# A block's softmax sums: scaling them on GpSimd six units earlier in its queue

## The chip, the cores and the metric

One core of a Trainium2 chip runs the whole kernel in one launch. The metric is the device time of the run in microseconds (us), here the median of three runs. The engines are TensorE (PE in the profile; its weight loads are PEld), VectorE (DVE), ScalarE (ACT), GpSimd (POOL) and SyncE (SP), which issues most of the DMAs. Each engine works through its own queue in order and waits there for semaphores of the others.

## The reference, cut to what matters

Three layers follow each other: attention with hash buckets, a mixture of experts with one expert for each token, and a SoLU layer. The change touches attention and the step from it to the experts.

```python
# attention: 2 batches x 8 heads, 768 positions, head size 64
mask = q_bucket[:, :, :, None] == k_bucket[:, :, None, :]
scores = np.where(mask, scale * q @ k.T, -1e9)
scores = scores - scores.max(-1, keepdims=True)
attn = np.exp(scores)
attn = attn / (attn.sum(-1, keepdims=True) + 1e-09)
x = attn @ v
# experts: 1536 tokens, width 512, 8 experts of width 1024
e_idx = argmax(x @ w_gate); out = gate_w * eom * (relu(x @ w1[e]) @ w2[e])
# SoLU: softmax-weighted hidden layer, layer norm, output matrix
```

## The kernel before

**Units and blocks.** Two heads form a pair (n = 0 to 7), and half of a pair's query rows form a block (j = 2n and 2n + 1, so 16 blocks). A unit is one tile of 128 query rows of one head; six units make a block, and 96 units (i = 0 to 95) make the attention loop at L976 to L996. Unit i works on the block i // 6.

**One unit.** TensorE makes the scores (`emit_s`, L558) and, in between, the transposes of the exponentials of two units earlier (`steps_t`, L597). VectorE takes the rows' maximum (`emit_max`, L568 to L572). ScalarE makes the exponential (`emit_exp`, L583), which adds up the row sums into `sums[j]`, and copies the transposes out of PSUM (L599). TensorE multiplies by v for the block before (`emit_pv`, L616).

**Background work.** Everything else hangs on a calendar written out by hand: `at(i, f, ...)` says that step f is issued in unit i, in slot 0 (behind the scores), slot 1 (behind the maximum) or slot 2 (at the unit's end). Steps with the same unit and slot are issued in the order in which they were registered. A step's place there is its place in each engine's queue.

**Finishing a block** takes these steps, counted from the block's first unit 6j: the unscaled output is read from PSUM into halves of 16 bits (`fin_hi` in 6j + 12, `fin_lo` in 6j + 13, slot 0); GpSimd adds 1e-9 to the sums and scales them into a small tile r (`fin_s`, L654, in 6j + 12, slot 2); VectorE takes the reciprocal of r (`fin_v`, L659, in 6j + 13, slot 1); TensorE multiplies by the gates (`fin_mm`, L673 to L675, in 6j + 15); VectorE scales the results with r (`fin_l`, L684, and `fin_x`, L695, in 6j + 16), and GpSimd splits the result into halves (L702, L704).

**Splitting q and k** of pair n is GpSimd's work too (`split`, L336 to L349): q is issued in unit 12(n - 1) - 1 and k in unit 12(n - 1), both in slot 2, one pair ahead of their use. SyncE's DMA transposes and copies follow (`trans`, L361, L367, L373), then TensorE's products for the buckets (`bits_a`, L509 to L515, q in 12(n - 1) + 5 and k in 12(n - 1) + 8). GpSimd further splits 16 pieces of the first experts' weights (`w_split`, L185 to L187), two in each pair. The splits are registered ahead of the finishing steps, so for even j from 0 to 10, where 6j + 12 is 12(n - 1) for n = j / 2 + 2, the queue of GpSimd has: split q, split k, `fin_s(j)`.

**The end of attention.** The last two blocks are finished by code written out behind the calendar: block 14 in units 93 and 94, block 15 in parts (query tiles 0 and 1, then 2) after the loop, at L999 to L1049. There `route_b` (L751) has GpSimd scatter three tokens' rows by indirect DMA (L762, L764), `fin_r` is `fin_s` followed by `fin_v`, and the router's steps (`route_a`, L713; `route_mm`, L732) and the gathering matmuls (`gather_mm`, L890) follow; the first expert begins on TensorE at L1143.

Of the kernel before, what the change touches and what calls it, by code (L numbers as in the profile page):

```python
# [8 lines left out]
F32 = mybir.dt.float32  # L9
# [12 lines left out]
def kernel(  # L22
# [15 lines left out]
    nc = tc.nc  # L38
# [7 lines left out]
    NP = B * HP  # L46
# [9 lines left out]
    X_S = 1024.0  # L56
    W_S = 2048.0
    G_S = 1024.0
    O_S = 16.0
# [158 lines left out]
    def setup_first():  # L218


        fi = const.tile([128, 3], F32, name="fi")
        io = const.tile([128, 1], I32, name="io")
        nc.gpsimd.iota(io, pattern=[[0, 1]], base=0, channel_multiplier=1)
        nc.gpsimd.memset(pw, 0.0)
        d = nc.vector
        d.tensor_scalar(out=io, in0=io, scalar1=31, scalar2=None, op0=ALU.bitwise_and)
        d.tensor_copy(out=fi[:, 0:1], in_=io)
        d.tensor_scalar(out=fi[:, 1:2], in0=fi[:, 0:1], scalar1=float(NBIT), scalar2=-TINY, op0=ALU.is_ge, op1=ALU.mult)
        d.tensor_scalar(out=fi[:, 2:3], in0=fi[:, 0:1], scalar1=float(2 * NBIT), scalar2=TINY, op0=ALU.is_ge,
                        op1=ALU.mult)  # L230
        d.tensor_copy(out=thr[:, 1:2], in_=fi[:, 1:2])
        d.scalar_tensor_tensor(out=thr[:, 0:1], in0=fi[:, 1:2], scalar=TINY, in1=fi[:, 2:3], op0=ALU.add, op1=ALU.add)
# [52 lines left out]
    def attention(es):  # L285
        def sbuf(name, bufs):
            return es.enter_context(tc.tile_pool(name=name, bufs=bufs))
# [9 lines left out]
        sm = sbuf("sm", 4)  # L297
# [16 lines left out]
        def at(i, f, *a, slot=2):  # L314
            bg.setdefault((i, slot), []).append((f, a))
# [231 lines left out]
        s_t, mx_t, p_t, pt, sums, pv, fin_t = {}, {}, {}, {}, {}, {}, {}  # L547
# [82 lines left out]
        lt_t = {}  # L630

        def fin_hi(j, q0=0, q1=3, on_act=False):
            if q0 == 0:
                xt = xp.tile([128, 2, SB], F16, tag="xt", name="xt")
                xf = xp.tile([128, 3, 128], F32, tag="xf", name="xf")
                r = sm.tile([128, 3, 2], F32, tag="r", name="r", bufs=2)
                fin_t[j] = lt_t[j], xt, xf, r
            o, i = fin_t[j][1][:, 0, q0 * 128:q1 * 128], pv[j, q0][:, 0:(q1 - q0) * 128]
            if on_act:
                nc.scalar.activation(out=o, in_=i, func=AF.Copy, scale=O_S)  # L640
            else:
                nc.vector.tensor_scalar(out=o, in0=i, scalar1=O_S, scalar2=None, op0=ALU.mult)
# [5 lines left out]
        def fin_a(j, q0=0, q1=3, on_act=False):  # L648
            fin_hi(j, q0, q1, on_act)
            fin_lo(j, q0, q1)  # L650

        def fin_s(j, q0=0, q1=3):
            r = fin_t[j][3][:, q0:q1]
            nc.gpsimd.tensor_scalar(out=r, in0=sums[j][:, q0:q1], scalar1=1e-9, scalar2=O_S / X_S,  # L654
                                    op0=ALU.add, op1=ALU.mult)

        def fin_v(j, q0=0, q1=3):
            r = fin_t[j][3][:, q0:q1]
            nc.vector.reciprocal(out=r, in_=r)  # L659

        def fin_r(j, q0=0, q1=3):
            fin_s(j, q0, q1)
            fin_v(j, q0, q1)
# [25 lines left out]
        def fin_x(j, q0=0, q1=3, on_act=False, on_dve=False):  # L689
# [13 lines left out]
                                        op0=ALU.mult, op1=ALU.mult)  # L703
            (nc.vector if on_dve else nc.gpsimd).tensor_tensor(out=x2[:, qs, 1, cs], in0=xf[:, qs], in1=x2[:, qs, 0, cs], op=ALU.subtract)  # L704

        fin_m = {}
        rts = {}
        parts = [(0, 3), (3, 3), (6, 3), (9, 2), (11, 1)]
# [189 lines left out]
        def gather_copy():  # L898
            xw = raw.tile([128, 1024], F32, tag="raw", name="raw").bitcast(F16)[:, 0:8 * CAP]
            xw = gx["xw"] = xw.rearrange("p (c n) -> p c n", c=8)  # L900
            for kk in range(4):
                nc.scalar.copy(out=xw[:, kk::4], in_=gx["ps"][kk][:, 0:2 * CAP].rearrange("p (a n) -> p a n", a=2))

        for n in range(1, NP):
            s0 = 12 * (n - 1)
            at(max(s0 - 1, 0), split, n, "q")
            at(s0, split, n, "k")
            at(s0 + 1, trans, n, "q")
            at(s0 + 3, trans, n, "k")
            if n + 1 < NP:  # L910
                at(s0 + 5, load, n + 1, "qk")
                at(s0 + 20, load, n + 1, "v")
            at(s0 + 5, bits_a, n, "q")
            at(s0 + 7, bits_b, n, "q", slot=0)
            at(s0 + 8, bits_a, n, "k", slot=0)
            at(s0 + 8, bits_b, n, "k", slot=1)
        JL = 2 * NP - 2
        for j in range(2 * NP):
            at(NU - 4 if j == JL else min(6 * j + 11, NU - 3), fin_pre, j)
        for j in range(JL):  # L920
            u = 6 * j + (13 if j == JL - 1 else 15)
            at(6 * j + 12, fin_hi, j)
            at(6 * j + 12, fin_s, j)
            at(6 * j + 13, fin_lo, j, slot=0)
            at(6 * j + 13, fin_v, j, slot=1)
            at(u, fin_mm, j)
            at(u + 1, fin_l, j, slot=0)
            at(u + 1, fin_x, j)
# [32 lines left out]
    with tc.manual_schedule():  # L961
        with ExitStack() as es:
            A = attention(es)
            pj = A["pj"]
            cm, rb, rg = A["cm"], A["rb"], A["rg"]
            setup_first()
            A["first"]()
            A["load"](1)
            setup_late()
            NU = A["NU"]  # L970
            bg = A["bg"]
            JL = 2 * NP - 2
            a_ = A.__getitem__
            pv, fa, tr = a_("emit_pv"), a_("fin_a"), a_("emit_t")
            due = a_("due")
            for i in range(NU):  # L976
                a_("emit_s")(i, a_("steps_t")(i - 2) if 2 <= i else iter(()))
                due(i, 0)
                a_("emit_max")(i)
                due(i, 1)  # L980
                a_("emit_exp")(i)
                jj, c = divmod(i - 8, 6)
                if 0 <= jj < JL and c % 2 == 0:
                    pv(jj, c)
                    pv(jj, c + 1)
                elif jj == JL and c < 2:
                    for x in range(3):
                        pv(JL, 3 * c + x)
                if i == NU - 3:
                    fa(JL, 0, 3, True)  # L990
                    a_("fin_r")(JL)
                if i == NU - 2:
                    a_("fin_mm")(JL)
                    a_("fin_l")(JL)
                    a_("fin_x")(JL)
                due(i, 2)  # L996
            assert not bg, bg.keys()

            J = JL + 1  # L999
            a_("route_a")(2)  # L1000
            tr(NU - 2)
            for c in range(3):
                pv(J, c, 0, 2)
            a_("route_mm")(2)
            a_("route_b")(2)
            for t in (6, 7, 8):
                a_("gather_oh")(t)
            for c in range(3, NS):
                pv(J, c, 0, 2)
            fa(J, 0, 2, True)  # L1010
            a_("fin_r")(J, 0, 2)
            a_("route_s")(2)
            tr(NU - 1)
            a_("fin_mm")(J, 0, 2)
            a_("fin_r")(J, 2, 3)
            for c in range(NS):
                pv(J, c, 2, 3)
            a_("fin_l")(J, 0, 2)
            a_("fin_x")(J, 0, 2, True)
            gm = a_("gather_mm")  # L1020
            a_("gather_ps")()
            a_("gather_first")((0, 1))
            for t in (6, 7):
                gm(t, (0, 1))
            a_("route_a")(3)
            a_("route_mm")(3, tail=True)
            fa(J, 2, 3, True)
            a_("route_b")(3)
            a_("gather_oh")(9)
            a_("fin_mm")(J, 2, 3)  # L1030
            a_("gather_first")((2, 3))
            for t in (6, 7):
                gm(t, (2, 3))
            a_("fin_l")(J, 2, 3)
            a_("route_a")(4)
            a_("route_mm")(4, (9, 10), True)
            for t in (8, 9):
                gm(t, range(4))
            a_("gather_oh")(10)
            gm(10, range(4))  # L1040
            a_("fin_x")(J, 2, 3, True, True)
            a_("route_b")(4)
            a_("gather_oh")(11)
            gm(11, range(4))
            a_("gather_copy")()
            a_("route_s")(3)
            a_("totals")()
            for x in range(3):
                a_("route_d")(x, 2, 3, 4)  # L1049
# [195 lines left out]
        for i, (kd, e, g) in enumerate(slots):  # L1245
# [18 lines left out]
            if kd == "m2" and 4 * e + g < NTILE:  # L1264
# [5 lines left out]
                    out=meta[:, :], out_offset=bass.IndirectOffsetOnAxis(ap=po, axis=0),  # L1270
# [161 lines left out]
```

## Time and profile before

| what | value |
|---|---|
| median of three runs | 562.01 us (560.13 to 562.04) |
| the profiled execution, whole time | 560.47 us |
| its span, first to last instruction | 558.7 us |
| TensorE busy | 507.0 us, 91% of the span |
| VectorE busy | 397.4 us, 71% |
| ScalarE busy | 340.2 us, 61% |
| GpSimd busy | 268.6 us, 48% |
| mean granted TensorE clock | 0.983 of full speed |

Busy time says how long an engine worked, not what bounds the kernel: attention fills the first half of the span, the experts and the SoLU layer the second, and their limits differ. Times of the trace are counted from the span's start. In a row of the timeline the first number is the start, the second the duration; a bracket at the end gives the idle time of the engine just before the row and, behind the arrow, what ended it.

### The profile page before, as it was taken

The page shows a single profiled execution, that of the slowest core. Times are in us where ns is not written, and L with a number is a line of the kernel's source. Part 1 is how long each engine was busy: PE and PEld are TensorE (multiplying, and loading weights), DVE is VectorE, ACT ScalarE, POOL GpSimd, SP SyncE. Part 2 cuts the span into 40 slices and gives each one's busy share as a digit, 9 for nine tenths or more (in the row PEclk, how much of TensorE's full clock was granted, in tenths as well). Part 3 has the DMA queues.
Part 4 walks back from the last instruction along what each step waited for, and adds up shares of the span by engine and source line. Part 5 has one row for each costly group of instructions (what it writes and reads, how often), then busy time and mean ns, then how long its engine had stood idle before and what let it go on. Part 6 is the DMA issues. An engine that isn't in the chain of part 4 may idle for free. (4 is left out here: it accounts for less than half of the span.)

```text
span 558.7 us, 10895 instructions
## 1 busy us (share of the span) xinstructions
PE 507.0 (91%) x3948; PEld 349.3 (63%) x3948; DVE 397.4 (71%) x892; ACT 340.2 (61%) x644; POOL 268.6 (48%) x355
## 2 busy tenths in 40 slices
PE   7798989899885989999799999969998999999995
PEld 5455646566553655665699999969994344444442
DVE  7866757666774866876579999999994885554530
ACT  6776767686683766886249687686652554442430
POOL 7985646676467766543528867321330112212131
PEclk9999989999998998999999999979999999999999
DMA  5577574744445442700599999999700245224251
GB/s 169 120 210 175 192 159 126 203 119 126 141 136 121 144 131 77 163 26 1 189 241 310 201 270 322 235 347 312 299 2 3 39 75 114 57 62 108 57 121 49
DMA packets 107177, 83.13 MB, mean 149 GB/s; under 512 B 80624, under 2 KB 89456, under 8 KB 107120
## 3 DMA queue, kind: packets, MB, share of 16 engines
q1 hardware_dynamic: 104816, 76.09, 51.1%
q0 software_dynamic: 2304, 6.31, 3.1%
q8 instruction: 32, 0.52, 0.4%
q14 instruction: 25, 0.20, 0.1%
HBM read 51.43 MB, written 9.97 MB: 110 GB/s over the span
## 5 line engine op out<-in xcount | busy, mean ns | idle before, releaser
L583 ACT ACTIVATE p<-s,mx 128x768 f32<-128x768 f32 x96 | 95.6, 996 | 64.4 <-DVE mx L572 46.1
L597 PE MATMUL t<-ident,p 128*128 128x128 f32 x576 | 128.1, 279 | 1.9 <-ACT pt L599 1.3
L568 DVE TENSOR_REDUCE mx<-s 128x1 f32<-128x768 f32 x96 | 91.3, 951 | 41.2 <-PE s L558 39.8
L597 PEld LDWEIGHTS t<-ident,p 128*128 128x128 f32 x576 | 78.8, 143 | 35.9 <-ACT pt L599 26.4
L599 ACT COPY pt<-t 128x384 f32<-128x384 f32 x192 | 85.4, 481 | 7.9 <-PE t L597 6.2
L558 PE MATMUL s<-k,q 128*128 128x384 f16 x192 | 60.0, 332 | 16.0 <-ACT p L583 16.0
L1154 POOL TENSOR_TENSOR hh<-hf,hh 128x448 f16<-128x448 f32 (+5 forms) x32 | 42.5, 1337 | 65.9 <-ACT hf L1153 65.8
L616 PE MATMUL v<-pt,v 128*64 128x384 f32 (+1 forms) x384 | 72.2, 500 | 1.2 <-DVE xt L646 1.2
L1298 PE MATMUL h<-wi,yT 128*128 128x512 f16 x288 | 63.8, 379 | 4.6 <-PEq L1103 2.6
L1174 PE MATMUL a<-hh,wb 128*128 128x224 f16 (+5 forms) x256 | 63.6, 251 | 0.0
L1175 PE MATMUL a<-hh,wb 128*128 128x224 f16 (+5 forms) x256 | 63.5, 251 | 0.0
L1176 PE MATMUL a<-hh,wb 128*128 128x224 f16 (+5 forms) x256 | 63.5, 251 | 0.0
L1366 PE MATMUL o<-wo,zT 128*128 128x512 f16 x288 | 63.5, 379 | 0.0
L1143 PE MATMUL a<-xw,wa 128*128 128x224 f16 (+5 forms) x224 | 56.0, 253 | 7.7 <-DVE yT L1184 6.7
L558 PE MATMUL s<-b,cm 128*128 128x384 f16 x192 | 58.2, 331 | 1.1 <-DVE b L521 1.1
L1144 PE MATMUL a<-xw,wa 128*128 128x224 f16 (+5 forms) x224 | 56.1, 254 | 0.0
L1145 PE MATMUL a<-xw,wa 128*128 128x224 f16 (+5 forms) x224 | 56.1, 254 | 0.0
L1298 PEld LDWEIGHTS <-yT 128*128 128x128 f16 x288 | 27.9, 98 | 39.0 <-DVE so L1325 3.2
L1366 PEld LDWEIGHTS <-zT 128*128 128x128 f16 x288 | 28.2, 98 | 34.0
L616 PEld LDWEIGHTS v<-pt,v 128*64 128x64 f32 x384 | 23.8, 138 | 27.6 <-issue 24.3
L1338 POOL TENSOR_TENSOR st<-st,nhalf 128x2 f32<-128x2 f32 x12 | 8.5, 706 | 66.1 <-DVE st L1337 65.9
L1314 ACT ACTIVATE ex<-h,st,csc 128x1024 f32<-128x1024 f32 x12 | 14.4, 1204 | 41.4 <-DVE st L1337 26.7
(266 smaller groups left out, 1043.6 us busy)
## 6 DMA issues: line engine op xcount, KB each, us to landing
raw<-in_moe_w_dram SPq DMA_DIRECT2D x64, 512.0 KB
raww<-in_moe_w_in_dram SPq DMA_DIRECT2D x8, 512.0 KB
raww<-in_moe_w_out_dram SPq DMA_DIRECT2D x8, 512.0 KB
xs<-raw SPq DMA_DIRECT2D x8, 448.0 KB
v<-in_v_dram SPq DMA_DIRECT2D x8, 384.0 KB
q<-in_q_dram SPq DMA_DIRECT2D x7, 384.0 KB
k<-in_k_dram SPq DMA_DIRECT2D x7, 384.0 KB
cm<-q SPq DMA_DIRECT2D x14, 96.0 KB
```

The lines of the kernel that those rows point to most:

```text
L558: nc.tensor.matmul(t[:, c, 0:SB], d[x, h][:, s], flat(d[y, h])[:, c * SB:(c + 1) * SB], start=first, stop=not first)
L568: nc.vector.tensor_reduce(out=mx[:, 0:1], in_=t[:, :, 0:SB], op=ALU.max, axis=AX.XY)
L583: nc.scalar.activation(out=p, in_=s_t.pop(i)[:, :, 0:SB], func=AF.Exp, scale=mx[:, 1:2], bias=mx[:, 2:3], accum_out=sums[j][:, qt, h:h + 1])
L597: nc.tensor.transpose(t[:, g * 128:(g + 1) * 128], p[:, c, g * 128:(g + 1) * 128], ident)
L599: nc.scalar.copy(out=pt[j, h][:, 3 * c:3 * c + 3, qt * 128:(qt + 1) * 128], in_=t[:, 0:SB].rearrange("p (g c) -> p g c", g=3))
L616: nc.tensor.matmul(pv[j, q0][64 * h:64 * h + 64, 0:w], vt[:, h, c], pt[j, h][:, c, q0 * 128:q1 * 128], start=(c == 0), stop=(c == NS - 1), ...
L1144: nc.tensor.matmul(ps[:, i, 0:n], w[:, 0, kk, fs], xw[:, KD + kk], start=False, stop=False)
L1174: nc.tensor.matmul(ps, w[:, 0, f, ds], hh[:, 0, f], start=(f == 0), stop=False)
L1175: nc.tensor.matmul(ps, w[:, 0, f, ds], hh[:, 1, f], start=False, stop=False)
L1176: nc.tensor.matmul(ps, w[:, 1, f, ds], hh[:, 0, f], start=False, stop=(f == KF - 1))
L1298: nc.tensor.matmul(ps[:, c], yT[:, a, kk, ts], w_i[:, w, kk, c * 512:(c + 1) * 512], start=(kk == 0 and a == 0 and w == 0), stop=(kk == KD ...
L1366: nc.tensor.matmul(ps, zT[:, KF * a + f], w_o[:, w, f], start=(f == 0 and a == 0 and w == 0), stop=(f == KF - 1 and a == 1))
```

## The change

`fin_s(j)` for blocks 0 to 14 moves on the calendar from unit 6j + 12 to unit 6j + 6, slot 2, and is registered ahead of the splits, so that it also comes first where unit and slot are the same. Its tile r is allocated there, with three buffers instead of two. `fin_s` of block 14 no longer stands beside its `fin_v` in unit 93 but in unit 90. For block 15 `fin_s` runs on VectorE instead of GpSimd, and its first part is issued ahead of the copies of `fa`. The reciprocal and all that reads it stay where they were.

```diff
@@ fin_hi @@
-                r = sm.tile([128, 3, 2], F32, tag="r", name="r", bufs=2)
-                fin_t[j] = lt_t[j], xt, xf, r
+                fin_t[j] = lt_t[j], xt, xf, r_t[j]
...
         def fin_s(j, q0=0, q1=3):
-            r = fin_t[j][3][:, q0:q1]
-            nc.gpsimd.tensor_scalar(out=r, in0=sums[j][:, q0:q1], scalar1=1e-9, scalar2=O_S / X_S,
+            if q0 == 0:
+                r_t[j] = sm.tile([128, 3, 2], F32, tag="r", name="r", bufs=3)
+            r = r_t[j][:, q0:q1]
+            (nc.vector if j == 2 * NP - 1 else nc.gpsimd).tensor_scalar(out=r, in0=sums[j][:, q0:q1], scalar1=1e-9, scalar2=O_S / X_S,
                                     op0=ALU.add, op1=ALU.mult)
...
         def fin_v(j, q0=0, q1=3):
-            r = fin_t[j][3][:, q0:q1]
+            r = r_t[j][:, q0:q1]
             nc.vector.reciprocal(out=r, in_=r)
...
+        JL = 2 * NP - 2
+        for j in range(JL + 1):
+            at(6 * j + 6, fin_s, j)
         for n in range(1, NP):
             s0 = 12 * (n - 1)
             at(max(s0 - 1, 0), split, n, "q")
...
             at(6 * j + 12, fin_hi, j)
-            at(6 * j + 12, fin_s, j)
...
                 if i == NU - 3:
                     fa(JL, 0, 3, True)
-                    a_("fin_r")(JL)
+                    a_("fin_v")(JL)
...
+            a_("fin_s")(J, 0, 2)
             fa(J, 0, 2, True)
-            a_("fin_r")(J, 0, 2)
+            a_("fin_v")(J, 0, 2)
```

## Rows read from the trace of the kernel before

**Rows 1.** Waits, whole span: who waited for whom, us in total, times, longest.
```profile
POOL xh L702 <- DVE xf L695: 65.1, 14, 7.0
...
DVE r L659 <- POOL r L654: 21.6, 6, 5.1
```
**Rows 2.** Timeline of one such wait, in the block of units 36 to 41: POOL, DVE, ACT.
```profile
103.73 0.83 POOL L336 TENSOR_SCALAR k<-k 128x768 f32<-128x768 f32 x1
...
108.10 0.20 POOL L654 TENSOR_SCALAR r<-sums 128x6 f32<-128x6 f32 x1
...
108.34 0.19 DVE L659 RECIPROCAL r<-r 128x6 f32<-128x6 f32 x1 [3.53 <-POOL r L654]
...
109.91 0.99 ACT L583 ACTIVATE p<-s,mx 128x768 f32<-128x768 f32 x1 [3.17 <-DVE mx L572]
```
**Rows 3.** Windows, one a block: length, then PE, PEld, DVE, ACT, POOL busy, clock, DMA.
```profile
38.97:54.76 15.79, 14.19 (x108) 8.88 (x105) 9.93 (x25) 11.54 (x25) 9.10 (x13) 1.00 0.82 183
54.76:68.59 13.83, 13.83 (x107) 8.90 (x105) 10.82 (x26) 10.95 (x24) 9.58 (x9) 1.00 0.57 191
68.59:86.72 18.13, 15.61 (x108) 9.59 (x105) 9.99 (x24) 11.72 (x25) 10.53 (x16) 0.91 0.77 189
...
100.56:117.42 16.86, 14.27 (x108) 8.89 (x105) 9.99 (x25) 11.52 (x25) 10.08 (x16) 1.00 0.69 183
...
163.68:186.20 22.52, 16.28 (x112) 9.77 (x109) 12.95 (x39) 11.73 (x25) 18.03 (x25) 0.92 0.57 151
186.20:200.03 13.83, 13.83 (x107) 8.90 (x105) 11.97 (x28) 10.95 (x24) 9.47 (x9) 1.00 0.36 121
200.03:218.73 18.70, 15.91 (x108) 9.35 (x105) 10.36 (x28) 11.84 (x27) 11.55 (x17) 0.91 0.42 103
...
232.58:245.94 13.36, 13.31 (x96) 8.67 (x93) 10.56 (x30) 11.08 (x24) 6.37 (x7) 1.00 0.52 98
```
**Rows 4.** The same columns for one microsecond behind two of the waits.
```profile
79.00:80.00 1.00, 0.95 (x3) 0.44 (x3) 0.61 (x3) 1.00 (x3) 0.00 (x0) 0.50 0.45 99
110.00:111.00 1.00, 0.00 (x0) 0.00 (x0) 0.93 (x3) 1.00 (x3) 0.00 (x0) 1.00 0.58 128
```
**Rows 5.** Timeline of PE and DVE in the block of units 60 to 65.
```profile
172.02 0.32 PE L558 MATMUL s<-k,q 128*128 128x384 f16 x1 [0.78 <-ACT p L583]
...
177.68 0.24 PE L673 MATMUL m<-rb,xt 128*128 128x160 f16 x1 [3.93 <-DVE rpr L758]
...
176.00 0.93 DVE L568 TENSOR_REDUCE mx<-s 128x1 f32<-128x768 f32 x1
```
**Rows 6.** Timeline of the end of attention: DVE, POOL, PE.
```profile
265.08 0.42 DVE L646 SCALAR_TENSOR_TENSOR xt<-v,xt 128x256 f16<-128x256 f32 x1 [0.94 <-ACT xt L640]
268.60 0.18 DVE L659 RECIPROCAL r<-r 128x4 f32<-128x4 f32 x1 [3.10 <-issue]
...
267.30 1.00 POOL L764 DMA_INDIRECT xs<-xh,slot_all  x1 [0.28 <-issue]
268.37 0.46 POOL L654 TENSOR_SCALAR r<-sums 128x4 f32<-128x4 f32 x2
...
271.13 0.18 PE L740 MATMUL v<-oh_all,upper 128*128 128x16 f16 x1 [2.45 <-DVE oh_all L727]
```
**Rows 7.** Timeline, what follows split k (SPq) and what uses it (PE).
```profile
109.83 2.58 SPq L373 DMA_TRANSPOSE b<-kl  x2
...
122.20 0.34 PE L515 MATMUL m<-b,pw 128*32 128x384 f16 x4
```
**Rows 8.** Timeline, the exponential of unit 23 (ACT) and GpSimd's split of q behind it.
```profile
69.53 0.19 ACT L583 ACTIVATION_READ_ACCUMULATOR p<-s,mx 128x1 f32 x1
...
69.70 1.79 POOL L342 TENSOR_TENSOR qs<-q,qs 128x384 f16<-128x384 f32 x2
```
**Rows 9.** Single lines: duration ns least/median/most, first and last start us, forms.
```profile
L570 DVE TENSOR_SCALAR mx<-mx x96: 153/153/156, 11.3 to 260.9; 128x1 f32<-128x1 f32 x96
...
L721 DVE SCALAR_TENSOR_TENSOR rne<-lg,rmx,iota_s x12: 213/227/885, 150.5 to 272.5; 128x8 f32<-128x8 f32 x12
```

More of the change, by code (lines that the diff above doesn't have):

```diff
@@ L704, in fin_x @@
             (nc.vector if on_dve else nc.gpsimd).tensor_tensor(out=x2[:, qs, 1, cs], in0=xf[:, qs], in1=x2[:, qs, 0, cs], op=ALU.subtract)
+        r_t = {}
         fin_m = {}
@@ L916, in attention @@
             at(s0 + 8, bits_b, n, "k", slot=1)
-        JL = 2 * NP - 2
         for j in range(2 * NP):
```

## The prediction

> **What bounds the kernel now.** I first read the waits of the whole span and looked for those that name the moved step. There is one: VectorE's reciprocal waits for GpSimd's step on the sums 6 times, 21.6 us in total, 5.1 us at the longest [rows 1]. Then I read the timeline around one of them [rows 2]. GpSimd begins with k at 103.73 and comes to the sums, 0.20 us of work, only at 108.10. VectorE stands still for 3.53 us before its reciprocal. Behind the reciprocal in VectorE's queue stands the next unit's maximum, so ScalarE's exponential starts 3.17 us late too, and TensorE, which needs that exponential out of its score buffer, runs dry behind them.
>
> Whether these stalls set the pace is seen in windows that each hold one block of six units [rows 3]. The second blocks of the pairs, where GpSimd has no split of q or k in front of the sums, take 13.83 us with TensorE busy for all of it (two such rows stand there, from 54.76 and 186.20; three more, from 86.72, 117.42 and 218.73, read 13.84, 13.83 and 13.85): there TensorE is the bound, at a clock of 1.00. The first blocks of pairs 1 to 6, each with one of the six waits, take 15.79, 18.13, 16.86, 16.86, 22.52 and 18.70 us (the fourth repeats the third, so one row stands for both) for nearly the same TensorE instructions (108 against 107; 112 in the fifth, which also routes tokens). The first block of pair 7 has nothing left to split, and takes 13.36 us, 13.31 of them busy, without the 12 small bucket products of the others. So a first block without the wait runs like a second block. Behind attention the experts start when its last step ends, and nothing of the change reaches into them; I take that half as shifted as a whole.
>
> **The change part by part.**
>
> *The move out of the split's way.* In first blocks the sums are now scaled six units, about 13.8 us, before the reciprocal, so the wait falls away. The gain of a block is its length less 13.83. Pair 1: 15.79 - 13.83 = 1.96. Pairs 3 and 4: 16.86 - 13.83 = 3.03 each. Pair 2: 18.13 - 13.83 = 4.30. Pair 6: 18.70 - 13.83 = 4.87, from which I keep back 0.2 for gating operations that only this block has, so 4.7.
>
> Pair 5 is read on its own, since there VectorE is late for a second reason, the router's work. The scores of unit 62 start only at 172.02 [rows 5], and four matmuls later, at about 173.4, the maximum can begin; in the trace it began at 176.00, right behind the reciprocal [rows 5]. The gain there is about 2.5 us, not the 5.1 of the wait, and TensorE's gap of 3.93 us before 177.68 [rows 5] shrinks to about 1.4. The rest is clock: TensorE is busy 16.28 us at a mean of 0.92 against 14.27 in the block of pair 3 [rows 3], some 1.9 us after 0.1 for four more matmuls. Sum 4.4.
>
> The blocks together: 1.96 + 4.30 + 3.03 + 3.03 + 4.4 + 4.7 = 21.4 us.
>
> Part of this is clock, not waiting. In pair 2 the granted clock is 0.50 (1.2 GHz instead of 2.4) at 79 to 80 us, after TensorE had run dry; in pair 3, after the same 3.5 us of VectorE's wait, it stays at 1.00 [rows 4]. By busy time the low clock costs 15.61 - 14.27 = 1.3 us in pair 2, 1.9 in pair 5 and 15.91 - 14.27 = 1.6 in pair 6 [rows 3], together 4.9. I take it as gone with the gaps, since the second blocks and that of pair 7, which have no such gap, ran at 1.00 [rows 3]; if it stayed, the gain would be 4.9 smaller. The Trainium skill ("TensorE: Matmul & The Clock Gate", section "HAM oscillation — how this bites in real kernels") says that idle gaps make the gate fall back to half rate and that the work behind them pays; the trace agrees in three of six gaps and shows that a gap need not do it. By that rule the dips go, and the sum stays as it is.
>
> A first block may settle elsewhere than at 13.83: TensorE's busy time in them at full clock is 14.19 to 14.27 [rows 3], up to 0.45 more, and the block of pair 7 needs 13.36. That is 6 x 0.45 = 2.7 us less gain or 6 x 0.47 = 2.8 us more. I take 13.83, the row with the same number of instructions.
>
> *What the moved step is moved past.* It has one instruction and issues no DMA. In first blocks it now stands behind one weight split and ahead of the next; for odd j it stands between split q and split k. There it newly waits for the last exponential of its own block. That wait could hold split k, on which SyncE's transposes, the bucket products and the next pair hang. Unit 23's exponential had delivered its sums at 69.72, while GpSimd was busy with split q until 71.49 [rows 8]: 1.8 us in hand, so no hold, 0. If there were one, the cover is wide: the second transpose of k ends at 112.41 and is used at 122.20 [rows 7], 9.8 us later, and the blocks shrink by 3 to 5. GpSimd's own idle time, 65.1 us in 14 waits for VectorE [rows 1], takes up small delays in the rest. The third buffer of r costs no time; r's reader of three blocks earlier has long finished.
>
> *The end of attention.* Block 15's sums were scaled by GpSimd behind three scatters, the last from 267.30 to 268.30; VectorE had ended its copy at 265.50 and sat idle 3.10 us until the reciprocal at 268.60 [rows 6]. On VectorE the step costs two instructions of some 0.15 us (the like of L570 [rows 9]), the first of them in idle time. The router's chain then starts about 2.8 us sooner, but TensorE, which waited 2.45 us for its result [rows 6], can give back no more than that: 2.45, say 2.4 us. GpSimd is free of its scatters at 268.30 and splits the block's result 2.0 us sooner than in the trace, which is before TensorE asks for it. Bounds: 0 if GpSimd's next scatters decide, 2.8 if TensorE were no limit.
>
> **Sum.** 21.4 + 2.4 = 23.8 us. The profiled execution took 560.47 us (span 558.7): 536.7 us. The median of the runs is 1.54 us above it, and the forecast is for a median: 562.01 - 23.8 = 538.2 us, 4.2% less.
>
> **The rivals.**
>
> *GpSimd trails.* With shorter blocks its queue has less room. In pair 3 it works 10.08 us in the first block and, as in the row from 54.76, some 9.6 in the second, 19.7 us of 30.7; in 27.7 us that still fits. In pair 5 it works 18.03 + 9.47 = 27.5 us [rows 3] of 36.4, and of about 32 after: if its scatters and splits come late there, pairs 5 and 6 keep what they lost, 4.4 + 4.7 = 9.1 us: 547.3 us.
>
> *VectorE is slowed beside the splits.* Before, it stood still during much of split k; now it works there. One of its lines, L721, took up to 885 ns instead of 213 while GpSimd split q [rows 9]. If the two small steps of each maximum (L570, L572) were stretched by the same 0.67 us in some two units of each of six splits, that is 2 x 2 x 6 x 0.67 = 16 us: 554 us. Against it: L570 takes 153 to 156 ns in all 96 units [rows 9], many of them beside a split of q. The Trainium skill ("GPSIMD Engine Reference", section "8. Key points") says that GpSimd shares its SBUF interfaces with VectorE and collides with instructions in a two-port mode or with two SBUF inputs; L721 bears that out, L570 does not.
>
> *Slower: the new wait holds split k.* Place: GpSimd's queue between split q and split k. A hold costs nothing until the 9.8 us of [rows 7], less some 3 us by which the block is shorter, are used up; beyond 6.8 us each further us delays the next pair by one. From a hold of about 10.8 us it eats the 4 us a pair that the change brings. At 12 us: 538.2 + 6 x 5.2 = 569 us. Against it stands the 1.8 us in hand [rows 8].
>
> *The change does not do what it says*, and the reciprocal still waits: only the end gains, 559.6 us.
>
> **How the numbers follow.** Forecast 538.2 with a chance of 0.80, within it clock dips that stay (543); GpSimd trails 0.10; VectorE slowed 0.04; no effect 0.03; slower 0.03. The range takes in 2.8 us more gain and a run at the lower end of the spread, 533, and reaches up to the trailing GpSimd, 547. A measurement of this kernel can tell about 0.5%, 2.8 us, from no change. Faster by more than that: 0.80 + 0.10 + 0.04 = 0.94; within it 0.03; slower 0.03.
>
> **What the profile after would show.** Right: no wait of the reciprocal for GpSimd in the list of waits; first blocks of pairs 1 to 4 and 6 within 0.5 us of 13.83 and TensorE busy throughout, at a clock of 1.00; pair 5 near 18.1; GpSimd's step on the sums directly behind a weight split or between split q and split k; in the end of attention the reciprocal right behind VectorE's copy, and TensorE's wait for the router gone. Wrong: first blocks above 15 us with TensorE waiting for a bucket product or its operands (GpSimd trails), L570 and L572 above 0.2 us (VectorE slowed), GpSimd idle in front of the sums for an exponential (the hold), or a clock of 0.5 in blocks without gaps.

## The result, and the profile after

The kernel after takes 536.55 us (median of four runs, 534.70 to 539.94) against 561.69 for the kernel before: a ratio of 0.956, 95% interval 0.951 to 0.962, so 25.1 us or 4.5% faster. The forecast was 538.2 with a range of 533 to 547. The profiled execution of the kernel after took 538.05 us (span 536.3).

In the kernel after, lines move a little: the step on the sums is L655 (L654 before), the reciprocal L660 (L659), the last of the block's steps L696 and L703 (L695 and L702), the experts' first matmul L1147 (L1143).

The wait list of the whole span no longer holds a wait of the reciprocal for GpSimd, which [rows 1] gave with 21.6 us. GpSimd's own waits for the blocks' results fell from the 65.1 us of [rows 1] to 43.1 (columns: us in total, times, longest):

```profile
POOL xh L703 <- DVE xf L696: 43.1, 13, 5.5
```

The timeline of the kernel after around the place of [rows 2], GpSimd and VectorE (columns: start, duration):

```profile
83.89 0.20 POOL L655 TENSOR_SCALAR r<-sums 128x6 f32<-128x6 f32 x1
...
95.53 1.79 POOL L342 TENSOR_TENSOR qs<-q,qs 128x384 f16<-128x384 f32 x2
...
97.57 0.20 POOL L655 TENSOR_SCALAR r<-sums 128x6 f32<-128x6 f32 x1
97.85 0.83 POOL L336 TENSOR_SCALAR k<-k 128x768 f32<-128x768 f32 x1
...
98.49 0.18 DVE L660 RECIPROCAL r<-r 128x6 f32<-128x6 f32 x1
```

The reciprocal at 98.49 belongs to block 4. Its sums were scaled at 83.89, 14.6 us sooner, and no bracket stands at its end: it waits for nothing. The row at 97.57 is the next block's step, between the split of q and the split of k, as the prediction placed it for odd j.

The windows of the kernel after for the first blocks of pairs 1 to 6, which answer to [rows 3], and from 136.39 the second block of pair 4 (columns as there: length, then PE, PEld, DVE, ACT, POOL busy, clock, DMA share, GB/s):

```profile
38.91:52.71 13.80, 13.80 (x107) 8.94 (x105) 9.93 (x24) 11.49 (x25) 8.93 (x13) 1.00 0.78 194
...
66.55:80.48 13.93, 13.88 (x108) 8.94 (x105) 10.02 (x24) 11.56 (x25) 9.96 (x16) 1.00 0.73 155
...
94.32:108.26 13.94, 13.89 (x108) 8.94 (x105) 10.01 (x25) 11.57 (x25) 10.06 (x16) 1.00 0.72 154
...
122.09:136.39 14.30, 14.25 (x110) 9.13 (x109) 10.01 (x24) 11.93 (x25) 10.43 (x16) 1.00 0.50 120
136.39:151.71 15.32, 13.81 (x109) 8.89 (x105) 12.69 (x39) 10.38 (x24) 8.87 (x12) 1.00 0.52 163
151.71:168.21 16.50, 14.42 (x112) 9.03 (x109) 12.87 (x39) 11.49 (x25) 15.00 (x21) 1.00 0.43 111
...
182.04:195.98 13.94, 13.89 (x108) 8.94 (x105) 11.19 (x29) 11.70 (x27) 10.04 (x16) 1.00 0.56 101
```

TensorE is busy for the whole length within 0.05 us in all first blocks but that of pair 5, and the clock is 1.00 in every row. The second block of pair 4 in the kernel before, which [rows 3] leaves out:

```profile
148.11:163.68 15.57, 13.99 (x111) 9.07 (x109) 12.63 (x39) 10.98 (x24) 9.12 (x12) 1.00 0.35 101
```

Set beside the prediction's terms:

| term | predicted | measured | from |
|---|---|---|---|
| pair 1 | 1.96 | 1.99 | 15.79 - 13.80 |
| pair 2 | 4.30 | 4.20 | 18.13 - 13.93 |
| pair 3 | 3.03 | 2.92 | 16.86 - 13.94 |
| pair 4 | 3.03 | 2.81 | 16.86 - 14.30, and 0.25 in the block behind (15.57 before, 15.32 after) |
| pair 5 | 4.4 | 6.02 | 22.52 - 16.50 |
| pair 6 | 4.7 | 4.76 | 18.70 - 13.94 |
| end of attention | 2.4 | 2.6 | what is left up to the first expert |
| sum, up to the first expert | 23.8 | 25.3 | 277.17 - 251.85 |

The experts' first matmul, in the kernel before and in the kernel after:

```profile
277.17 0.26 PE L1143 MATMUL a<-raw,wa 128*128 128x224 f16 x1 [0.67 <-ACT raw L902]
```
```profile
251.85 0.26 PE L1147 MATMUL a<-raw,wa 128*128 128x224 f16 x1 [0.67 <-ACT raw L904]
```

It comes 25.3 us sooner, but the span is only 22.4 us shorter (558.7 to 536.3): from there to the end it was 281.5 us before and 284.5 after. Whether the faster attention lengthens the experts, or the experts vary by themselves, was the first thing to find out.

### The profile page after: what moved, and what is told of

Same layout as the page of the kernel before. It is cut to its first block, busy times and chain, and to the rows that moved or that the text cites. A ratio compares the mean times of both kernels' runs of the same rounds, so it can differ in the third digit from the quotient of the medians.

```text
span 536.3 us, 10907 instructions
## 1 busy us (share of the span) xinstructions
PE 499.2 (93%) x3948; PEld 346.8 (65%) x3948; DVE 398.6 (74%) x894; ACT 339.7 (63%) x644; POOL 269.8 (50%) x353
## 5 line engine op out<-in xcount | busy, mean ns | idle before, releaser
L597 PE MATMUL t<-ident,p 128*128 128x128 f32 x576 | 126.0, 275 | 1.6 <-ACT pt L599 1.0
L597 PEld LDWEIGHTS t<-ident,p 128*128 128x128 f32 x576 | 77.7, 141 | 20.7 <-ACT pt L599 12.4
L1158 POOL TENSOR_TENSOR hh<-hf,hh 128x448 f16<-128x448 f32 (+5 forms) x32 | 45.2, 1422 | 67.4 <-ACT hf L1157 67.3
L616 PE MATMUL v<-pt,v 128*64 128x384 f32 (+1 forms) x384 | 70.8, 492 | 1.2 <-DVE xt L645 1.2
L1147 PE MATMUL a<-xw,wa 128*128 128x224 f16 (+5 forms) x224 | 56.1, 253 | 10.6 <-DVE yT L1188 9.3
L616 PEld LDWEIGHTS v<-pt,v 128*64 128x64 f32 x384 | 23.5, 136 | 26.8 <-issue 22.4
```

Source lines behind the costliest of these rows:

```text
L597: nc.tensor.transpose(t[:, g * 128:(g + 1) * 128], p[:, c, g * 128:(g + 1) * 128], ident)
L616: nc.tensor.matmul(pv[j, q0][64 * h:64 * h + 64, 0:w], vt[:, h, c], pt[j, h][:, c, q0 * 128:q1 * 128], start=(c == 0), stop=(c == NS - 1), ...
L1147: nc.tensor.matmul(ps[:, i, 0:n], w[:, 0, kk, fs], xw[:, kk], start=(kk == 0), stop=False)
```

## The experiments

Diffs are against the kernel after, unless the text says otherwise. The kernel before ran on the same chip beside each of them, and its median there stands in brackets.

**The kernel after, twice more.**

> The changed kernel once more, beside its parts. Its first expert began at 251.85 us in the first profile, 25.3 us sooner than before (277.17), but the span ended only 22.4 us sooner. If the expert phase simply varies by 2 to 3 us from one execution to the next, the first expert begins again within 0.3 us of 251.9 while the rest of the span lies between 279 and 285 us. If the shorter attention makes the expert phase itself longer, the rest is again about 284.4 us, 2.9 more than the 281.5 of before. Median 534 to 540 us.

> The kernel after once more, beside the other two on the same chip: 537 us, between 535 and 539, since the expert phase differs between executions by some microseconds.

Measured: 536.95 us (before: 561.99), ratio 0.956 [0.954, 0.958], and on another chip 537.37 (561.31), ratio 0.958 [0.955, 0.961]. The first expert begins at 253.76 and 251.74, and from there to the end it is 281.2 us (span 535.0) and 282.6 (span 534.3). The first of these runs missed the expected 251.9 by 1.9 us: 1.0 us in the blocks of pair 5, told below under that pair, and 0.9 between unit 90 and the first expert (29.54 us for 28.66). Over all profiles here this stretch lies between 281.2 and 286.3 us, with no order by how long attention took (281.5 in the kernel before, 284.4 in the slowest kernel below). So the 2.9 us by which the span gained less than attention are a difference between executions; the experts were shifted as a whole. What makes the stretch vary is only known in part. TensorE is busy in it for 262.2 us in the kernel before and in the first run of the kernel after, at a mean clock of 0.98 in both, so these 2.9 us are idle time. But the two longest stretches of all, 286.3 and 285.8 us, have more busy time (264.0 and 263.5 us, clock 0.98 and 0.97) than the shortest, 281.2 us (261.7 us, clock 0.99).

**Only the calendar move; block 15's step stays on GpSimd.**

```diff
-            (nc.vector if j == 2 * NP - 1 else nc.gpsimd).tensor_scalar(out=r, ...
+            nc.gpsimd.tensor_scalar(out=r, ...
```

> The calendar move alone: block 15's sums stay on GpSimd. Theory (six stalls in the attention loop, and apart from them the end): the loop is as in the changed kernel (unit 90's maximum at about 223.2 us), the reciprocal of block 15 again waits some 3 us behind the three scatters, and the first expert begins about 2.6 us later than 251.9, at 254.5; median about 539. Rival (the end gains nothing by itself, GpSimd's scatters decide there): first expert at 251.9, median as the changed kernel.

Measured: 539.40 us (561.99), ratio 0.960 [0.957, 0.963]. The loop runs as in the kernel after (unit 90 begins at 224.30, in the second run of the kernel after at 224.22). At the end of attention the old wait is back; VectorE in the timeline:

```profile
246.97 0.18 DVE L660 RECIPROCAL r<-r 128x4 f32<-128x4 f32 x1 [3.11 <-issue]
```

This is the row of [rows 6] again, 3.11 us of idle time for 3.10. Between the medians the end is worth 2.45 us. The profile, of the slowest of the six executions, does not give it cleanly: the first expert begins at 256.55, not at the expected 254.5, and from unit 90 to there it is 32.25 us, where the kernel before has 31.23 with the same wait. Behind TensorE's wait of 2.47 us for the router the granted clock is 0.50 here from 250.3 to 253.3; in the kernel before, behind the 2.45 us of [rows 6], it stayed at 1.00. The kernel after takes 28.66 and 28.59 us for this stretch in its first and third run.

**Only the end: the kernel before, with block 15's step on VectorE.** The diff is against the kernel before.

```diff
-            nc.gpsimd.tensor_scalar(out=r, in0=sums[j][:, q0:q1], ...
+            (nc.vector if j == 2 * NP - 1 else nc.gpsimd).tensor_scalar(out=r, ...
```

The step stays in `fin_r`, behind the copies of `fa`; only the kernel after has its first part ahead of them.

> The end alone: block 15's sums on VectorE, the calendar as before. Theory: the six waits of 2.5 to 5.1 us are all there, the first expert begins at 277.2 - 2.6 = 274.6 us, median about 559, no more than 0.5% below before. Rival (the loop and the end are not independent): anything beyond 1 us away from that.

Measured: 559.31 us (561.99), ratio 0.995 [0.992, 0.997], 2.7 us. The calendar move alone gave 22.6 us; the two parts add up to 25.3, and the whole change gave 25.0 on this chip. All six waits are there, but the windows of pairs 2 and 6 are not those of [rows 3]:

```profile
68.36:85.20 16.84, 14.27 (x108) 8.88 (x105) 9.99 (x24) 11.51 (x25) 10.06 (x16) 1.00 0.77 169
...
162.16:185.03 22.87, 16.30 (x112) 9.64 (x109) 12.95 (x39) 11.73 (x25) 18.38 (x25) 0.93 0.58 156
...
198.87:215.93 17.06, 14.28 (x108) 8.88 (x105) 10.37 (x29) 11.75 (x27) 10.06 (x16) 1.00 0.47 113
```

In the same place, behind the same 3.52 and 3.50 us of wait, the clock stays at 1.00, and the blocks take 16.84 and 17.06 us for the 18.13 and 18.70 of [rows 3]. So the same wait can pass without a dip. The dip in pair 5, behind 5.11 us, came again (0.93). These two blocks, 2.9 us together, are why the first expert begins at 271.76 and not at the expected 274.6. But the profiled execution was the fastest of its twelve (556.11 us, median 559.31), so it does not say how often the dips stay away; more on this under the clock, below. The end is clean here: from unit 90, at 243.13, to the first expert it is 28.63 us, 2.6 less than the 31.23 of the kernel before and the same as in the kernel after (28.66). So the place ahead of the copies adds nothing that shows; the other engine is what counts.

**Only the order, not the six units.** The step stays in unit 6j + 12, but is registered ahead of the splits.

```diff
-            at(6 * j + 6, fin_s, j)
+            at(min(6 * j + 12, 90), fin_s, j)
```

> The sums at the old unit 6j + 12, but registered ahead of the splits, so that they stand between split q and split k instead of behind both. If only the place in GpSimd's queue matters, they run where split q ends, which in the changed kernel is 0.9 to 2.2 us before the reciprocal in five of the six blocks and 0.6 us after it in the block of pair 5: one short wait of about 0.8 us, median 0 to 1.5 us above the changed kernel, first expert at 252 to 253.5. If the six units of distance matter, the waits come back in part: two or more waits of over 1 us, first expert above 255.

Measured: 538.45 us (561.99), ratio 0.958 [0.956, 0.961]; its interval overlaps that of the kernel after on the same chip. Two short waits are left in the whole trace, where one was expected:

```profile
159.57 0.19 DVE L660 RECIPROCAL r<-r 128x6 f32<-128x6 f32 x1 [0.75 <-POOL r L655]
...
174.85 0.19 DVE L660 RECIPROCAL r<-r 128x6 f32<-128x6 f32 x1 [1.27 <-POOL r L655]
```

The first block of pair 5 takes 17.74 us (without any wait of the reciprocal it took 16.50, but 17.65 in the second run of the kernel after), the other first blocks 13.81 to 13.94. So the gain comes from the place in GpSimd's queue, ahead of the split; six units of lead are a margin that only the neighbourhood of pair 5 uses, where GpSimd also scatters tokens, and what that is worth lies below what the runs tell apart.

**The step on VectorE, in its old unit, in all blocks.** This takes GpSimd out of the chain altogether.

```diff
-            (nc.vector if j == 2 * NP - 1 else nc.gpsimd).tensor_scalar(out=r, ...
+            nc.vector.tensor_scalar(out=r, ...
...
-            at(6 * j + 6, fin_s, j)
...
+            at(6 * j + 12, fin_s, j)
             at(6 * j + 12, fin_hi, j)
...
                 if i == NU - 3:
+                    a_("fin_s")(JL)
```

> All blocks' sums on VectorE at the old unit 6j + 12, none on GpSimd. Theory (the wait for GpSimd's queue was the cost, not the operation): no wait for GpSimd is left, VectorE does 15 more operations of 0.15 to 0.2 us, some 2.5 us in all, mostly in its idle time: first expert at 251.9 to 253.5, median 536 to 539. Rival (VectorE is itself short of time in the first blocks): 2.5 us or more are lost, first expert at 254.4 or later.

Measured: 541.95 us (560.19), ratio 0.967 [0.965, 0.969]. There is no wait for GpSimd, yet it is slower than the kernel after and than the 536 to 539 us expected; the first expert begins at 257.11, past the 254.4 of the rival, though most is lost in the second blocks and not in the first. The first blocks are as there (13.80 to 13.95 in pairs 1 to 4), but the second blocks of pairs 1, 2, 3 and 6 take 14.68 to 14.97 us in place of 13.84. Seventeen steps take 159 ns at least, 823 in the median and 1950 at most, where GpSimd needs 188 to 207 for them in the kernel before. One of them, with GpSimd beside it:

```profile
53.60 2.14 POOL L187 TENSOR_TENSOR wa<-raw,wa 128x1024 f16<-128x1024 f32 x1
...
53.98 1.79 DVE L655 TENSOR_SCALAR r<-sums 128x6 f32<-128x6 f32 x1
```

Six elements a row take 1.79 us, and they end at 55.77, as GpSimd's operation does (55.74). The same is true of all the long ones: of the fifteen steps on six elements thirteen begin while GpSimd is at work, and each ends within 0.1 us of the end of the GpSimd instruction that it began beside, be it one with two inputs (L187, L342) or with one (L185, L186); the two others, with GpSimd idle, take 0.16 us. VectorE is held by GpSimd there, at 0.8 to 1.1 us for a second block. The Trainium skill ("GPSIMD Engine Reference", section "8. Key points") says that GpSimd shares its SBUF interfaces with VectorE and collides with instructions in a two-port mode or with two SBUF inputs. The trace agrees that VectorE can be held; the step has one input, and in which mode it ran no row shows.

**The old place for three of the six, twice.** One kernel keeps blocks 2, 8 and 10 in their old place (waits in pairs 2, 5 and 6), the other blocks 0, 4 and 6 (waits in pairs 1, 3 and 4).

```diff
+        LATE = (2, 8, 10)
...
-            at(6 * j + 6, fin_s, j)
+            if j not in LATE:
+                at(6 * j + 6, fin_s, j)
...
+            if j in LATE:
+                at(6 * j + 12, fin_s, j)
```

> The changed kernel with the sums of blocks 2, 8 and 10 back behind the splits: those are the waits in the first blocks of pairs 2, 5 and 6, the three after which the clock fell. If the gains of the blocks add up, what returns is 4.2 + 6.0 + 4.8 = 15.0 us: first expert at 266.9, the other first blocks at 13.8 to 14.3 us. If the low clock belongs to these gaps, it is seen in these three blocks and in no other of the loop; if it falls where it likes, the three blocks together vary by 1.3 us and more for each dip that stays away.

> The changed kernel with the sums of blocks 0, 4 and 6 back behind the splits: the waits in the first blocks of pairs 1, 3 and 4, after which the clock did not fall. If the gains add up, 2.0 + 2.9 + 2.8 = 7.7 us return: first expert at 259.6, clock 1.00 all through the loop. If a dip follows such a gap by chance, one or two of pairs 3 and 4 show a clock of about 0.9 in their first block and 1.3 us more each: 260.9 to 262.2.

Measured: 551.87 us and 546.03 (both 560.19), ratios 0.985 [0.983, 0.988] and 0.974 [0.972, 0.976]. The first expert begins at 266.0 and 262.0. The windows of the three waiting blocks of each, blocks 2, 8 and 10 first, then blocks 0, 4 and 6:

```profile
66.56:83.92 17.36, 14.27 (x107) 8.88 (x105) 9.98 (x24) 11.53 (x25) 10.51 (x17) 1.00 0.83 197
...
155.15:179.06 23.91, 17.46 (x112) 10.17 (x109) 12.95 (x39) 11.75 (x25) 19.25 (x27) 0.86 0.59 164
...
193.25:210.23 16.98, 14.00 (x105) 8.68 (x101) 10.32 (x28) 11.53 (x27) 9.98 (x16) 1.00 0.46 113
```
```profile
38.92:54.84 15.92, 14.19 (x108) 8.87 (x105) 9.93 (x25) 11.55 (x25) 9.15 (x14) 1.00 0.80 200
...
96.46:115.30 18.84, 15.91 (x108) 9.50 (x105) 10.00 (x25) 11.63 (x25) 11.56 (x18) 0.91 0.66 182
...
129.14:146.34 17.20, 14.27 (x108) 8.89 (x105) 9.99 (x25) 11.53 (x25) 10.35 (x17) 1.00 0.57 157
```

The first blocks without a wait take what they take in the kernel after (13.81 to 13.95 us, and 16.49 in pair 5), the others about what they took before, give or take a dip of the clock: each block pays for its own wait. Up to the first expert 14.2 us return with blocks 2, 8 and 10 (15.0 expected) and 10.2 with blocks 0, 4 and 6 (7.7 expected): the waits are 0.1 to 0.5 us longer than in the kernel before, and in pair 3 a dip adds 1.6 us (15.91 - 14.27). Pair 3, which held 1.00 in [rows 3], falls to 0.91 here, and pairs 2 and 6 hold 1.00. Counted over the kernel before and the three kernels that keep such waits: behind waits of 3.5 to 4.0 us of the reciprocal the clock fell in 3 of 12 blocks, behind 5.1 to 5.4 us (pair 5) in 3 of 3, behind 2.4 to 2.6 us (pair 1) in none of 3. The first blocks without such a wait kept 1.00 in all kernels.

**The slower rival: split k made later.** Ten passes over k (8.3 us expected, 9.1 in its trace) go in front of every split of k, and then, in another kernel, five (4.5 us in its trace) in front of those of pairs 2 to 7. The passes multiply k by one, in place, in both kernels; there is no scratch tile.

```diff
+            if nm == "k":
+                for _ in range(10):
+                    g.tensor_scalar(out=x, in0=x, scalar1=1.0, scalar2=1.0, op0=ALU.mult, op1=ALU.mult)
```

> The changed kernel with ten more GpSimd passes over k (0.83 us each, 8.3 us) in front of every split of k; the values stay the same. It puts the hold of split k to the test that the prediction priced at nothing up to 6.8 us. In the changed kernel the last transpose of k ends 6.1, 6.0, 7.0, 3.7 and 5.8 us before its use in pairs 2 to 6. By that cover 8.3 us cost about 2.2 + 2.3 + 1.3 + 4.6 + 2.5 = 13 us: first expert at about 265, with TensorE waiting in the units of the bucket products of k. If the splits were still on the path as they stand, the whole 6 x 8.3 = 50 us come on top; if GpSimd's queue has far more room than that, nothing does.

> The kernel after with five extra passes of GpSimd over a scratch tile, some 4.15 us by the length of the same pass in pad8, in front of the splitting of k of pairs 2 to 7, and none in pair 1. Theory: in the kernel after the last transpose of k ends 3.7 to 7.0 us before its first use, so 4.15 us lie inside that cover in all pairs but one, where 0.5 us stick out; the time is that of the kernel after, 537 us, to 0.5 us above it. Rival: the splitting is on the path already, and all of the extra shows: six times 4.15 us, 25 us, so 562.

Measured with ten passes: 569.28 us (560.19), ratio 1.016 [1.013, 1.018], slower than the kernel before; the first expert begins at 282.62, not at 265. The first blocks stay at 13.80 to 13.94 us in pairs 1 to 4 and 6; the second blocks grow over those of the kernel after by 1.4, 5.8, 2.8, 1.0, 7.5 and 3.3 us, and the start, where the split of pair 1 has hardly any cover (0.7 us in the kernel after), by 9.4, which the expectation had left out; a low clock is part of that (0.50 from 35 to 40 us). Two of the second blocks, those of pairs 2 and 5:

```profile
91.17:110.81 19.64, 16.32 (x108) 9.41 (x105) 10.91 (x27) 10.96 (x24) 16.47 (x19) 0.91 0.57 152
...
188.24:209.61 21.37, 16.65 (x108) 9.51 (x105) 11.12 (x28) 10.95 (x24) 19.50 (x23) 0.84 0.64 186
```

The second blocks sum to 21.8 us, not to the 13 expected. Both rows hold a dip of the clock (0.91 and 0.84); by busy time, against the 14.68 of pair 3's, they account for 1.6 and 2.0 us of the difference. The passes are also longer than expected, and the second block of pair 1 was left out of the expectation. By the covers of the kernel after (7.2, 6.1, 6.0, 7.0, 3.7 and 5.8 us in the second blocks of pairs 1 to 6) 9.1 us cost 18.8 us in all, and 21.8 less the 3.6 of clock is 18.2. Block by block the fit is looser: pair 2 pays 4.2 us without its dip for 3.0 by this count, pair 4 1.0 for 2.1.

Measured with five passes: 539.66 us (561.31), ratio 0.961 [0.959, 0.964], 2.3 us above the kernel after on the same chip where 0 to 0.5 were expected, and 3.0 at unit 90 (226.14 to 223.15). Pairs 1 to 3 show nothing of it (second blocks 13.84). Pairs 4, 5 and 6 pay 1.26, 0.74 and 0.96 us. In the timeline of pair 4's second block (the first two rows) and of pair 6's:

```profile
138.29 2.13 POOL L187 TENSOR_TENSOR wa<-raw,wa 128x1024 f16<-128x1024 f32 x1
138.41 2.34 DVE L726 SCALAR_TENSOR_TENSOR rne<-lg,rmx,iota_s 128x8 f32<-128x8 f32 x3
...
199.76 2.58 SPq L376 DMA_TRANSPOSE b<-kl  x2
...
203.71 0.34 PE L518 MATMUL m<-b,pw 128*32 128x384 f16 x2 [0.64 <-DMA b<-kl]
```

In pairs 5 and 6 TensorE waits for the transpose of k, 0.42 and 0.64 us: the cover is used up. In pair 6 that comes at less than the 5.8 us counted: SyncE's row ends at 202.34, and the matmul that waits for the transfer starts only at 203.71, so a cover counted to the end of SyncE's row is 1.4 us too wide there. In pair 4 it is not the transpose. A GpSimd operation has slid onto VectorE's routing step, whose three instructions take 2.34 us here and 1.08 in the kernel after (third run):

```profile
138.41 1.08 DVE L723 SCALAR_TENSOR_TENSOR rne<-lg,rmx,iota_s 128x8 f32<-128x8 f32 x3
```

So the cover of split k is real, some 4 to 7 us by pair when counted so, and what a late GpSimd costs depends on what it then runs beside.

**What is left in the kernel after: the router's steps further apart.** TensorE's largest gaps in pairs 4 and 5 of the kernel after wait for the router's work on VectorE:

```profile
144.27 0.17 PE L742 MATMUL m<-oh_all,upper 128*128 128x24 f16 x1 [1.46 <-DVE raw L537]
157.56 1.51 PE L616 MATMUL v<-pt,v 128*64 128x384 f32 x8 [1.20 <-DVE xt L645]
160.03 0.32 PE L558 MATMUL s<-k,q 128*128 128x384 f16 x1 [0.78 <-ACT p L583]
```

```diff
-        for x, f, g in ((6, route_a, 0), (8, route_mm, 0), (8, route_b, 0), (12, route_s, 0),
-                        (12, route_a, 1), (14, route_mm, 1), ...
+        for x, f, g in ((8, route_a, 0), (11, route_mm, 0), (11, route_b, 0), (12, route_s, 0),
+                        (13, route_a, 1), (14, route_mm, 1), ...
```

> The kernel after with three steps of the router spread further apart in the calendar: the first half's first step from unit 54 to 56, its matmuls from 56 to 59, the second half's first step from 60 to 61. Theory: TensorE is the bound of the loop now, and the router's two blocks hold the largest gaps that are left in it, waits of 1.46, 1.20 and 0.78 us; apart, the steps wait less, and the time is 1.5 to 2.5 us below the kernel after, 534.5 to 535.5 us. Rival: the gaps only move with the steps, and the time is that of the kernel after, 537.

Measured: 534.70 us (561.31), ratio 0.952, within what was expected and 2.7 us (0.5%) below the kernel after on the same chip; the intervals of the two ratios only just part (0.9490 to 0.9548 and 0.9549 to 0.9613). Of the three gaps one of 0.54 us is left, and the blocks are these:

```profile
136.43:150.80 14.37, 14.20 (x109) 8.87 (x105) 13.11 (x39) 10.62 (x25) 9.32 (x10) 1.00 0.43 149
150.80:166.01 15.21, 14.53 (x112) 9.00 (x109) 11.76 (x39) 11.44 (x25) 13.35 (x21) 1.00 0.62 139
```

They took 15.30 and 16.49 us in the kernel after, while the next is 0.34 longer here (14.19 for 13.85). Unit 90 begins 2.1 us sooner, so the gain in attention carries through to the time. This version beats both kernels, the kernel after by little.

## Why the prediction was right, step by step

**What bounds the kernel.** Right. Without the wait, first blocks run like second blocks, with TensorE busy throughout. The terms of pairs 1, 2, 3 and 6 fit within 0.11 us, since 13.83 was a row of this kernel for the same number of TensorE instructions. The two kernels with three waits each show that these terms are each block's own. The measured median lies 1.65 us below the forecast of 538.2: 1.3 us of gain, for which pair 5's 1.6 would do, and 0.3 because the median before was 562.01 then and 561.69 beside this result.

**Pair 5** is the term that was mis-sized: 4.4 predicted, 6.02 measured. The failed step is the reading of [rows 5]. I took the matmuls at 172.02 for the scores of unit 62, so that its maximum could not begin before 173.4. They are the scores of unit 63: the bracket names an exponential, that of unit 61, which frees the score buffer. The scores of unit 62 had been done long since, and the maximum could follow the reciprocal at once. In the kernel before, the last matmul of the scores of unit 62 and, behind it, the maximum of unit 61:

```profile
167.67 0.33 PE L558 MATMUL s<-b,cm 128*128 128x384 f16 x1
...
169.41 0.94 DVE L568 TENSOR_REDUCE mx<-s 128x1 f32<-128x768 f32 x1
```

VectorE in the timeline of the kernel after:

```profile
157.43 0.94 DVE L568 TENSOR_REDUCE mx<-s 128x1 f32<-128x768 f32 x1
...
158.72 0.18 DVE L660 RECIPROCAL r<-r 128x6 f32<-128x6 f32 x1
158.82 0.92 DVE L568 TENSOR_REDUCE mx<-s 128x1 f32<-128x768 f32 x1
```

From the maximum of unit 61 to that of unit 62 it is 1.39 us here and was 6.6 before, so the whole wait of 5.1 us came back, not the 2.5 of the prediction. TensorE's idle time in the block fell by 4.16 us, from 22.52 - 16.28 = 6.24 to 16.50 - 14.42 = 2.08, of which the router's 1.20 and 0.78 us, above, are nearly all. Its busy time fell by 1.86 us, the clock's part, for which the prediction had 1.9. In two other executions of this loop the block took 17.65 and 17.68 us. VectorE's maximum of unit 66 begins 1.2 us late there; in the first and in the second run of the kernel after:

```profile
168.21 0.96 DVE L568 TENSOR_REDUCE mx<-s 128x1 f32<-128x768 f32 x1 [0.62 <-PE s L558]
```
```profile
169.37 0.96 DVE L568 TENSOR_REDUCE mx<-s 128x1 f32<-128x768 f32 x1 [1.76 <-PE t L597]
```

TensorE's rows ahead of it start within 0.02 us of the same times in both, and the trace names no cause; this stays open. Of the extra time 1.0 us is left at the end of the next block.

**Pair 4** gave 2.81 for 3.03, 2.56 of it in its first block and 0.25 in the block behind. Why 0.2 us are missing no run shows.

**The clock.** The prediction counted 4.9 us of dips into the gain. In the profiled pair of executions this was right: all three are gone. Which block dips is not fixed: behind VectorE's waits of 3.5 to 4.0 us it was 3 of 12, and TensorE's idle time in these blocks does not tell them apart (length less busy time: 2.5, 2.8 and 2.9 us with a dip, 2.6 to 3.1 without). The Trainium skill ("TensorE: Matmul & The Clock Gate", section "HAM oscillation — how this bites in real kernels") says that idle gaps bring the fall; the traces agree in all three blocks of pair 5 that keep the wait, and show in the others that a gap need not do it.

For a typical execution the 4.9 us are not shown to be too much. Traces exist of one execution each, but the mean granted clock of every execution is known. It is 0.983 in the profiled execution of the kernel before, with its three dips, and 0.9825 in the median of the 34 others beside the experiments; in the kernel after it is 0.992 in the median of 15. With only the end changed, the profiled execution, which lacks two of the dips, has 0.989, and the median of its twelve has 0.982. So a typical execution of the kernel before lost about as much to the clock as the profiled one; in which blocks, no trace shows. The dips were rightly part of the gain, and 25.3 us in the profiles up to the first expert agree with 25.1 between the medians.

**What the step is moved past.** Right, and now measured. In all of the kernel after, GpSimd waits once for an exponential in front of the sums:

```profile
211.03 0.20 POOL L655 TENSOR_SCALAR r<-sums 128x6 f32<-128x6 f32 x1 [1.81 <-ACT p L583]
```

That is in pair 7's first block, behind which no split follows. The cover of split k was read too wide in one respect: 9.8 less 3, that is 6.8 us, from pair 3 alone. In the kernel after the last transpose of k ends, by SyncE's row, 3.7 us ahead of its use in pair 5, and with 4.5 us of delay TensorE waits:

```profile
166.68 2.65 SPq L373 DMA_TRANSPOSE b<-kl  x2
...
172.99 0.34 PE L515 MATMUL m<-b,pw 128*32 128x384 f16 x4
```

It decided nothing, since there was no hold.

**The end of attention.** Predicted 2.4, measured 2.6 in the profiles (31.23 us from unit 90 to the first expert before, 28.66 after, and 28.63 with the end alone changed), 2.45 and 2.7 between medians when it was left out or made alone. In the kernel after, the rows that answer to [rows 6]:

```profile
241.28 0.16 DVE L655 TENSOR_SCALAR r<-sums 128x4 f32<-128x4 f32 x1
...
242.65 0.17 DVE L660 RECIPROCAL r<-r 128x4 f32<-128x4 f32 x1
...
245.75 0.17 PE L742 MATMUL v<-oh_all,upper 128*128 128x16 f16 x1
...
247.84 0.18 PE L742 MATMUL v<-oh_all,upper 128*128 128x8 f16 x1 [0.54 <-DVE oh_all L729]
```

The reciprocal no longer waits, and TensorE's wait of 2.45 us for the router is gone; one of 0.54 us for the next part came up.

**The rivals.** GpSimd did not trail: no block but pair 5's is above 15 us among the first ones, and GpSimd waits 43.1 us for VectorE in the list of waits, so it has room. VectorE was not slowed in the kernel after: L570 takes 153 to 156 ns in all 96 units, as in [rows 9]. But the mechanism of that rival exists here: on VectorE the moved step itself takes up to 1.95 us, held by GpSimd, and one instruction of the routing step up to 2.03 with five passes in front of split k. What kept it out, as far as these rows show, is which instructions run beside GpSimd in the kernel after, not that there is no such effect. The slower rival was not reached; its price is there, and ten passes make the kernel slower than before.

## What to carry to other kernels

A small step that stands behind a long one in an in-order queue costs its consumer the long one's length; look for it as a wait of a fast engine for a 0.2 us instruction, and read what the releasing engine did right before. It is enough to issue it ahead of the long step once its input is there; handing it to the consumer's engine instead can cost more, if that engine is held beside the first one's work. Read the gain of a repeated block from a sibling block of the same trace that lacks the wait, and keep clock dips as a term of their own, since another execution may not have them.

## What the runs showed of the hardware that was not expected

A VectorE instruction on six elements a row took 0.16 us with GpSimd idle and up to 1.95 us when it began beside a GpSimd instruction, of one input or two: in 13 of 13 cases it ended with that instruction. VectorE's one-element step L570 stayed at 153 to 156 ns in all 96 units of the same trace. The granted clock fell behind the same wait in the same block in one execution and held in another: 3 of 12 behind VectorE's waits of 3.5 to 4.0 us; at the end of attention it fell behind 2.47 us of TensorE's own waiting and held behind 2.45. The stretch from the first expert to the end varied from 281.2 to 286.3 us over executions with the same instructions there.
